# Transposing the exponentials of causal attention in two halves of 56 query rows, with padded queries and a new ranking of the work

## The chip, the cores and the metric

One NeuronCore of a Trainium2 chip runs the whole program. The metric is the device time of one execution in microseconds (us); the time before the change is 591.86 us, the median of three runs (591.3 to 592.4). One execution was also recorded by the hardware profiler, and the rows below come from it.

## The reference

Three stages follow one another: causal attention of 2 batches, 12 heads, 448 tokens and 64 features a head; a feed-forward layer with a rational function; and a gated feed-forward layer. The change sits in the first.

```python
scores = scale * np.matmul(q, k.transpose(0, 1, 3, 2))      # 448 x 448 a head
scores = np.where(mask, -1000000000.0, scores)              # causal
attn = np.exp(scores - np.max(scores, axis=-1, keepdims=True))
attn = attn / (np.sum(attn, axis=-1, keepdims=True) + 1e-09)
x = np.matmul(attn, v)                                      # 896 tokens x 768 in all
h = x @ w_in                                                # 768 x 2048
...
x = P(h) / (Q(h) + 1e-6) @ w_out                            # 2048 x 768
out = (sigmoid(x @ w_gate) * (x @ w_val)) @ w_out2          # 768 x 1536, 1536 x 768
```

## The kernel before, in words

**Attention** goes through 12 pairs of heads. A pair's queries and keys lie side by side as `qk` (128 partitions: 64 features of one head, 64 of the other), loaded on SP's queue at L558. The 448 queries of a pair are cut into NQ = 4 tiles t of CP = 112, and these into three groups k: tiles 0 and 1, tile 2, tile 3. Because of the causal mask tile t meets (t + 1) x 112 keys.

For each group, `scores` (L566) multiplies 112 queries with the keys for both heads j. A head's 64 features fill one half of the rows of TensorE (PE), so the two heads' matmuls stand in different halves by rows, and they write to two PSUM banks (`ps[:, 0]` and `ps[:, 1]`). A full fp32 matmul is issued as two instructions, each with a weight load of its own; a transpose as one. `maximum` (L579) is a DVE operation that adds the mask, writes the negated scores to SBUF as `e` and keeps their minimum; `exponentials` (L594) turns `e` into exponentials on ACT, with their sum. `turn` (L606) transposes `e` on PE block by block: for a tile t and a head j there are t + 1 blocks of 112 x 112, each one transpose (L615) over all 112 query rows, 20 for a pair. `copied` (L617) brings the transposed blocks from PSUM to SBUF as `pt`, on ACT for tile 2 and on DVE for the others. `values` (L646) multiplies `v` with `pt`; the two heads' results stand in two halves of PE's columns. `factors` (L627) spreads the inverse sums over the partitions with a matmul against the identity, also in two halves by columns, and `result` (L664) applies them. `xh` and `xl` (L667, L670) are two parts of the result whose sum has fp32's accuracy; the layers that follow multiply with fp32r parts, three matmuls for one product.

So PE works in three ways of division: rows (scores), columns (values and factors) and whole (the transposes, and all matmuls of the layers, L260 to L262, L319 to L321, L458 to L460 and L512 to L514).

**Order.** Nothing is ordered by hand. Each step is a `Job` with an engine, a cost, the jobs that it depends on and a rank. `in_turn` (L36) plays these jobs through with their costs, takes on each engine the ready job of the lowest rank, and writes the instructions out in that order; each engine then executes its own in that fixed order. Ranks come from `R` (offsets by kind of job, L692), costs from `C`, `EXP`, `MAX`, `COPY`, and the cost of a group's transposes is 0.2 us for each (t + 1) and 0.1 more (L728). `MODES` (L695) says which PE jobs divide the array; `switch` is the cost of going from one division to another, and it is 0 here. The first layer's products for the first batch (L260 to L262, then L319 to L321) are jobs of the same plan and fill gaps of the attention.

When the last job of the attention is done, `late` (L764) gives its SBUF and PSUM room to the layers: `room_b`, and the banks `ps_b` and `ps_d`. Weights come packed over SP's queue, are unpacked by ACT (L165, L169) and DVE (L172; L395 for the second layer), split on POOL (L180, L184, L423), and land in `room_a`, `room_b` and the `oh`/`ol` tiles. Ahead of the gated layer, DVE forms sums of the activations (L431 to L437, `act_sum`) and of the weights (L409 to L413, `weight_sums`), since that layer's products are formed with seven multiplications in place of eight.

Of the kernel before, what the change touches and what calls it, by code (L numbers as in the profile page):

```python
# [8 lines left out]
F32 = mybir.dt.float32  # L9
# [3 lines left out]
ALU = mybir.AluOpType  # L13
# [58 lines left out]
def tile_causal_attention__moe_rational__moe_glu(  # L72
# [13 lines left out]
    nc = tc.nc  # L86


    B, NP, P, _, S = qk.shape
    CP, NQ, _, D = v.shape[2:]  # L90
    DM = NP * P
    KC = DM // P

# [7 lines left out]
    MASK = -8.0e9  # L101
# [4 lines left out]
    const = ctx.enter_context(tc.tile_pool(name="const", bufs=1))  # L106
# [13 lines left out]
    for i in range(N_WARM):  # L120
        nc.tensor.matmul(warm[:, : 2 * P], ones[:, :P], ones, start=True, stop=True)

    ident = const.tile([P, P], F32, name="ident")
    make_identity(nc, ident)
    mask = const.tile([CP, S], F32, name="mask")
    nc.gpsimd.memset(mask, 0.0)
    nc.gpsimd.affine_select(
        out=mask[:, S - CP :],
        in_=mask[:, S - CP :],
        compare_op=ALU.is_ge,  # L130
        fill=MASK,
        base=0,
        pattern=[[-1, CP]],
        channel_multiplier=1,
    )
    a_sb = const.tile([P, 4], F32, name="a_sb")
    b_sb = const.tile([P, 2], F32, name="b_sb")
    nb = const.tile([P, 2], F32, name="nb")
# [14 lines left out]
    def weight(dst, src, nm, beside):  # L153

        f = src.shape[-1]
        raw = raws.tile([P, 2 * DM], U32, tag="raw", name=f"raw_{nm}")
        nc.sync.dma_start(out=raw.rearrange("p (c f) -> p c f", f=f), in_=src)
# [12 lines left out]
        yield  # L170
        val = raws.tile([P, DM], U32, tag="val", name=f"val_{nm}")
        nc.vector.scalar_tensor_tensor(  # L172
# [31 lines left out]
    def rows(tiles, key, src, f):  # L204


        def dst():
            tiles[key] = [
                wo_p.tile([P, DM], F32R, tag=t, name=f"{t}_{key[0]}{key[1]}_{key[2]}") for t in ("oh", "ol")
            ]  # L210
# [9 lines left out]
    BY_VECTOR = ("t3",)  # L220
    NO = DM // 2
    BY_POOL = ("in", "out")
    YW = 4 * DM
    ypools = [y_a, None]
# [83 lines left out]
    def out1_tile(c, b, e):  # L308
# [37 lines left out]
        "p6": ("s2", "t2", "B", True),  # L346
        "p7": ("s3", "t3", "C", True),
        "p5": ("s1", "t1", "D", True),
# [182 lines left out]
    nat = att.enter_context(tc.tile_pool(name="nat", bufs=3))  # L531
    xn_p = att.enter_context(tc.tile_pool(name="xn", bufs=1))
    ep = att.enter_context(tc.tile_pool(name="ep", bufs=2))
    pp = att.enter_context(tc.tile_pool(name="pp", bufs=2))
    st = att.enter_context(tc.tile_pool(name="st", bufs=3))
    ps_s = att.enter_context(tc.tile_pool(name="ps_s", bufs=2, space=PSUM))
# [6 lines left out]
    GROUPS = [(0, 1), (2,), (3,)]  # L543

    PK = NQ - 1
    NB = PK * PK + NQ

    def cols_of(t):

        grp = next(grp for grp in GROUPS if t in grp)  # L550
        return sum((k + 1) * CP for k in grp if k < t), (t + 1) * CP

    def load(n):
        b, hp = pairs[n]
        d = T[n] = {}
        u = f"{b}_{hp}"
        d["qk"] = nat.tile([P, 2, S], F32, tag="qk", name=f"qk_{u}")
        nc.sync.dma_start(out=d["qk"], in_=qk[b, hp])  # L558
        d["v"] = nat.tile([CP, NQ, 2, D], F32, tag="v", name=f"v_{u}")
        nc.sync.dma_start(out=d["v"], in_=v[b, hp])  # L560

        d["sum"] = st.tile([CP, NQ, 2], F32, tag="sum", name=f"sum_{u}")
        d["sc"] = st.tile([CP, NQ, 2], F32, tag="sc", name=f"sc_{u}")
        d["pt"] = pp.tile([CP, 2, NB, CP], F32, tag="pt", name=f"pt_{u}")

    def scores(n, k):  # L566

        d = T[n]
        ps = d["s", k] = ps_s.tile([CP, 2, 512], F32, tag="s", name=f"s_{n}_{k}")
        for t in GROUPS[k]:  # L570
            o, nk = cols_of(t)
            c = slice(t * CP, (t + 1) * CP)
            for j in range(2):
                r = slice(j * D, (j + 1) * D)
                nc.tensor.matmul(  # L575
                    ps[:, j, o : o + nk], d["qk"][r, 0, c], d["qk"][r, 1, :nk], start=True, stop=True
                )

    def maximum(n, k, t, j):  # L579
        d = T[n]  # L580
        o, nk = cols_of(t)
        e = d["e", t, j] = ep.tile([CP, nk], F32, tag=f"e{t}", name=f"e_{n}_{t}_{j}")
        nc.vector.tensor_tensor_reduce(  # L583
            e,
            d["s", k][:, j, o : o + nk],
            mask[:, S - nk :],
            op0=ALU.add,
            op1=ALU.min,
            scale=SCALE,
            scalar=3.0e38,  # L590
            accum_out=d["sc"][:, t, j : j + 1],
        )
# [12 lines left out]

    def turn(n, k):  # L606
        d = T[n]
        pz = d["p", k] = ps_s.tile([CP, 2, 512], F32, tag="s", name=f"p_{n}_{k}")
        for t in GROUPS[k]:
            o, _ = cols_of(t)  # L610
            for j in range(2):
                for kt in range(t + 1):
                    at = slice(o + kt * CP, o + (kt + 1) * CP)
                    e = d["e", t, j][:, kt * CP : (kt + 1) * CP]
                    nc.tensor.transpose(pz[:, j, at], e, ident[:CP, :CP])  # L615

    def copied(n, k, t):  # L617
        d = T[n]
        o, nk = cols_of(t)
        src = d["p", k][:, :, o : o + nk].rearrange("p j (k c) -> p j k c", c=CP)  # L620
        dst = d["pt"][:, :, t : t * (PK + 1) + 1 : PK]
        if t == 2:
            nc.scalar.copy(dst, src)
        else:
            nc.vector.tensor_copy(dst, src)

    def factors(n):  # L627

        d = T[n]
        d["r"] = ps_r.tile([P, 512], F32, tag="r", name=f"r_{n}")[:, :S]  # L630

        for i in range(NQ):
            for j in range(2):
                nc.tensor.matmul(
                    d["r"][j * D : (j + 1) * D, i * CP : (i + 1) * CP],
                    d["sum"][:, i, j : j + 1].to_broadcast([CP, D]),
                    ident[:CP, :CP],
                    start=True,
                    stop=True,
                )  # L640
# [5 lines left out]
    def values(n, kt):  # L646

        d = T[n]
        if kt == 0:
            d["x"] = ps_x.tile([P, 512], F32, tag="x", name=f"x_{n}")[:, :S]  # L650
        for j in range(2):
            nc.tensor.matmul(
                d["x"][j * D : (j + 1) * D, kt * CP :],
                d["v"][:, kt, j],
                d["pt"][:, j, kt * (PK + 1) : kt * PK + NQ].rearrange("p k c -> p (k c)"),
                start=(kt == 0),
                stop=(kt == NQ - 1),
            )
# [30 lines left out]

    NG = len(GROUPS)  # L690
    LA = 2
    R = dict(s=-41.5, turn=-13.0, r=-20.0, x=34.0, w=-3.5, max=-15.5, copy=-9.5, inv=7.0, xn=12.5, rout=-42.5, exp=6.75, hi=1.0, lo=4.5, e=3.0, p1=12.0, ts=0.0, th=-12.0, tl=0.0, wh=0.0, w2=-1.5, sum=6.0)  # L692
    C = dict(w_at=9.0, w_step=5.0, s=0.3, p=0.1, x=0.15, max=0.08, exp=0.19, switch=0.0, stay=0, copy=0.0, wa=0.1, wd=0.2, xn=0.1, rat=0.2)
    H = dict(PE=0.2, DVE=0.1, ACT=0.12, POOL=0.12, SP=0.03)
    MODES = {"s": "rows", "x": "columns", "r": "columns"}  # L695
    EXP = (0.39, 0.48, 0.57, 0.67)
    MAX = (0.28, 0.39, 0.51, 0.62)
    COPY = (0.39, 0.62, 0.70, 1.09)
# [1 line left out]
    for it in range(len(pairs) * NG + LA):  # L700
        n, k = divmod(it, NG)
        rank = it * NQ / NG
        if n < len(pairs):
            if k == 0:
# [5 lines left out]
                [("load", n), *freed_by("s")],  # L710
                rank + R["s"],
                scores,
# [3 lines left out]
            for t in GROUPS[k]:  # L716
                for j in both:
                    job(("max", n, t, j), "DVE", MAX[t] + C["max"], [("s", n, k), ("p", n - 1, k)], rank + R["max"], maximum, n, k, t, j)
                    job(("exp", n, t, j), "ACT", EXP[t] + C["exp"], [("max", n, t, j), ("r", n - 3)], rank + R["exp"], exponentials, n, t, j)
            freed["s"].append([("max", n, t, j) for t in GROUPS[k] for j in both])  # L720
        if it < LA:
            continue
        n, k = divmod(it - LA, NG)
# [1 line left out]
        job(  # L725
            ("p", n, k),
            "PE",
            sum(0.2 * (t + 1) for t in GROUPS[k]) + C["p"],  # L728
            [("exp", n, t, j) for t in GROUPS[k] for j in both] + freed_by("s"),
            rank + R["turn"],  # L730
            turn,
            n,
            k,
# [125 lines left out]
    at = {"end": 1000.0}  # L859
# [203 lines left out]
    u = 3  # L1063
# [30 lines left out]
def _laid_out(inputs):  # L1094
    import numpy as _np

    q, k, v = (inputs[n] for n in "qkv")
    b, h, s, d = q.shape
    t = [a.reshape(b, h // 2, 2, s, d).transpose(0, 1, 2, 4, 3).reshape(b, h // 2, 2 * d, s) for a in (q, k)]
    arrays = {  # L1100
        "qk": _np.ascontiguousarray(_np.stack(t, axis=3)),
        "v": _np.ascontiguousarray(v.reshape(b, h // 2, 2, 4, s // 4, d).transpose(0, 1, 4, 3, 2, 5)),
    }
    for name in _WEIGHTS:
        a = _np.ascontiguousarray(inputs[name])

        arrays[name] = a.view(_np.int64) if a.dtype == _np.float64 else a
    return arrays
# [22 lines left out]
```

## Time and profile before

| | us |
|---|---|
| median of three runs | 591.86 |
| the profiled execution, its own time | 591.18 |
| its span, from the first to the last instruction | 589.4 |
| PE busy | 576.6 |
| DVE busy | 441.7 |
| ACT busy | 388.3 |
| POOL busy | 320.6 |

The profiled execution's time holds 1.8 us around its span. A busy time counts the stretches in which at least one instruction of the engine is recorded as running. Matmuls overlap, and their ends are modelled, so two neighbouring starts tell more of PE's pace than a mean duration does. "PEld" is PE's weight load, which runs beside its matmuls; "issue" and a name behind "<-" in brackets say what ended an engine's idle time.

### The profile page before, as it was taken

Reading aid. Unit: us, or ns where it says so; the run is one execution under the profiler, and the core shown is the slowest. Engines: PE = TensorE matmul, PEld = TensorE weight load, DVE = VectorE, ACT = ScalarE, POOL = GpSimd, SP = SyncE. Lnnn points to the kernel's source line nnn. Section 1 sums busy time; section 2 is a strip of 40 time slices with the busy share of each in tenths; the row PEclk is TensorE's granted clock in tenths of the full one; section 3 lists DMA queues with packets and bytes.
Section 4 is the critical chain, followed back from the end, with each engine's and each line's share of the span. In section 5 each row is a group of like instructions: output and inputs, shape, how many; then the busy total and the mean of one; then the engine's idle time right before and its main releaser. Section 6 shows DMA issues by size and latency. Waiting matters only on the chain.

```text
span 589.4 us, 9051 instructions
## 1 busy us (share of the span) xinstructions
PE 576.6 (98%) x3244; PEld 497.3 (84%) x3244; DVE 441.7 (75%) x814; ACT 388.3 (66%) x767; POOL 320.6 (54%) x259
## 2 busy tenths in 40 slices
PE   7999999999999999999999979999999999999997
PEld 5556666689988998899889859999999999999996
DVE  4877889945978868789788987547668876857547
ACT  6888888957997673877677366677646566547210
POOL 0543341176647464636377887766658745756410
PEclk9999999999999999999999999999999999999999
DMA  7554450045333132513131103522443235441105
GB/s 247 191 197 126 147 179 17 2 158 165 108 107 108 54 108 73 191 59 107 55 108 54 55 0 108 160 87 82 154 131 137 85 131 161 125 138 60 53 2 187
DMA packets 35245, 65.07 MB, mean 110 GB/s; under 512 B 2368, under 2 KB 22592, under 8 KB 35200
## 3 DMA queue, kind: packets, MB, share of 16 engines
q1 hardware_dynamic: 35200, 64.50, 33.1%
q8 instruction: 25, 0.41, 0.3%
q14 instruction: 20, 0.16, 0.1%
HBM read 61.74 MB, written 2.75 MB: 109 GB/s over the span
## 4 chain that ended last, share of the span: by engine, by line
PE 66%; DVE 5%; ACT 3%; DMA 2%; POOL 1%; issue 1%; ACTq 0%; POOLq 0%; DVEq 0%
PE z L512 5%; PE z L514 5%; PE z L513 5%; PE o L320 5%; PE o L321 5%; PE o L319 5%; PE h L262 4%; PE h L261 4%; PE h L260 4%; PE u_C L458 2%; PE u_C L459 2%; PE u_C L460 2%; PE u_D L460 2%; PE u_D L459 2%; PE u_D L458 2%; PE u_A L460 2%
## 5 line engine op out<-in xcount | busy, mean ns | idle before, releaser
L184 POOL TENSOR_TENSOR ol_out<-val_out,oh_out 128x768 fp32r<-128x768 f32 x28 | 52.9, 1890 | 6.9 <-ACT oh_out L182 5.5
L512 PE MATMUL z<-oh_out,room_b 128*128 128x384 f32 x168 | 56.3, 335 | 0.0
L514 PE MATMUL z<-oh_out,room_b 128*128 128x384 f32 x168 | 56.1, 334 | 0.0
L513 PE MATMUL z<-ol_out,room_b 128*128 128x384 f32 x168 | 56.1, 334 | 0.0
L423 POOL TENSOR_TENSOR room_a<-val,room_a 128x384 fp32r<-128x384 f32 x30 | 34.1, 1146 | 40.4 <-ACT room_a L419 40.4
L597 ACT ACTIVATE e<-e,sc 112x112 f32<-112x112 f32 (+3 forms) x96 | 49.7, 520 | 6.5 <-DVE sc L583 6.4
L522 DVE TENSOR_TENSOR y<-y,z 128x384 f32<-128x384 f32 x84 | 43.5, 550 | 9.6 <-PE z L514 9.6
L583 DVE CUSTOM_DVE_ANT_0 e<-s,mask 112x112 f32<-112x112 f32 (+3 forms) x96 | 38.2, 445 | 14.4 <-PE s L575 13.1
L293 POOL TENSOR_TENSOR room_a<-t_h,room_a 128x384 fp32r<-128x384 f32 (+1 forms) x16 | 19.7, 1232 | 52.5 <-ACT room_a L291 46.0
L423 POOL TENSOR_TENSOR room_a<-raw,room_a 128x384 fp32r<-128x384 f32 x38 | 45.0, 1201 | 5.4 <-ACT room_a L419 5.4
L172 DVE SCALAR_TENSOR_TENSOR val_out<-raw_out 128x768 uint32<-128x768 uint32 x28 | 34.7, 1241 | 10.7 <-ACT raw_out L169 5.6
L395 DVE SCALAR_TENSOR_TENSOR val<-raw 128x768 uint32<-128x768 uint32 x24 | 25.1, 1044 | 22.3 <-ACT raw L392 19.1
L293 POOL TENSOR_TENSOR room_b<-t_h,room_b 128x512 fp32r<-128x512 f32 (+1 forms) x16 | 20.7, 1291 | 34.7 <-ACT room_b L291 33.8
L320 PE MATMUL o<-room_b,oh_out 128*128 128x512 f32 (+1 forms) x96 | 36.9, 385 | 0.7 <-POOL room_b L293 0.7
L319 PE MATMUL o<-room_b,oh_out 128*128 128x512 f32 (+1 forms) x96 | 36.9, 384 | 0.3 <-ACT room_b L291 0.3
L321 PE MATMUL o<-room_b,ol_out 128*128 128x512 f32 (+1 forms) x96 | 36.8, 384 | 0.0
L260 PE MATMUL h<-xh,room_a 128*128 128x448 f32 (+2 forms) x96 | 36.5, 380 | 0.0
L261 PE MATMUL h<-xl,room_a 128*128 128x448 f32 (+2 forms) x96 | 34.9, 364 | 0.0
L262 PE MATMUL h<-xh,room_a 128*128 128x448 f32 (+2 forms) x96 | 34.9, 363 | 0.0
L165 ACT ACTIVATE raw_out<-raw_out 128x768 f32<-128x768 f32 x28 | 25.6, 916 | 14.0 <-DMA raw_out<-in_moe_w_out_dram 13.8
L260 PE MATMUL h<-xh,room_b 128*128 128x384 f32 (+1 forms) x96 | 34.7, 362 | 0.0
L262 PE MATMUL h<-xh,room_b 128*128 128x384 f32 (+1 forms) x96 | 34.7, 362 | 0.0
(175 smaller groups left out, 1882.0 us busy)
## 6 DMA issues: line engine op xcount, KB each, us to landing
raw_out<-in_moe_w_out_dram SPq DMA_DIRECT2D x28, 768.0 KB, 4.3
raw_in<-in_moe_w_in_dram SPq DMA_DIRECT2D x16, 768.0 KB, 4.6
raw<-in_moe_w_gate_dram SPq DMA_DIRECT2D x24, 384.0 KB, 3.3
raw<-in_moe_w_val_dram SPq DMA_DIRECT2D x24, 384.0 KB, 4.0
qk<-in_qk_dram SPq DMA_DIRECT2D x12, 448.0 KB, 5.8
v<-in_v_dram SPq DMA_DIRECT2D x12, 224.0 KB, 3.6
out_dram<-y SPq DMA_DIRECT2D x14, 192.0 KB, 1.9
a_sb<-in_moe_a_dram SPq DMA_DIRECT2D x1, 2.0 KB, 7.7
```

Of the source, the lines that this page charges most:

```text
L184: nc.gpsimd.tensor_tensor(lo, vf, hi, op=ALU.subtract)
L260: nc.tensor.matmul(ps, hi[:, c, fs], xh[:, c, bs], start=(c == 0), stop=False)
L261: nc.tensor.matmul(ps, hi[:, c, fs], xl[:, c, bs], start=False, stop=False)
L262: nc.tensor.matmul(ps, lo[:, c, fs], xh[:, c, bs], start=False, stop=(c == KC - 1))
L319: nc.tensor.matmul(ps, hi[:, es], gh, start=(i == 0), stop=False)
L320: nc.tensor.matmul(ps, hi[:, es], gl, start=False, stop=False)
L321: nc.tensor.matmul(ps, lo[:, es], gh, start=False, stop=(i == NF - 1))
L423: nc.gpsimd.tensor_tensor(lo, halves[u, PRODUCTS[name][0]], hi, op=ALU.subtract)
L512: nc.tensor.matmul(ps, gh[:, ms], hi[:, ns], start=(u == us[0]), stop=False)
L513: nc.tensor.matmul(ps, gh[:, ms], lo[:, ns], start=False, stop=False)
L514: nc.tensor.matmul(ps, gl[:, ms], hi[:, ns], start=False, stop=(u == us[-1]))
L597: nc.scalar.activation(e, e, AF.Exp, bias=d["sc"][:, t, j : j + 1], scale=-1.0, accum_out=d["sum"][:, t, j : j + 1])
```

## The change

- A transpose of a block over 112 query rows becomes two, each over 56 rows: rows 0 to 55 and rows 64 to 119. The two stand in PE's two halves by rows. The first half writes to one PSUM bank of the tile, the second to the other; the two heads share each bank (`pz`, four slots of 256 columns). There are now 40 transposes for a pair in place of 20, and each passes 56 columns of the identity in place of 112.
- For that the second half's queries must begin at partition 64: a query tile has PQ = 120 rows, of which rows 56 to 63 are padding. The host writes zeros there; `qk` grows from 896 to 928 columns. Score weights, `e`, the sums and the mask have 120 rows; the mask is cut by two operations on POOL in place of one.
- `pt` keeps its size; its blocks are ordered by block, half, head and 56 queries in place of head and block, so `copied` reads four slots of PSUM, `values` reads runs of 56 columns, and `factors` multiplies with two runs of 56 columns of the identity.
- The plan: nearly all of the offsets `R` are changed, some costs `C` and hand-over times `H`, `switch` goes from 0 to 0.05, the transposes count as divided by rows like the scores, and their cost is 0.14 us for each (t + 1) and 0.1 more.

```diff
-    mask = const.tile([CP, S], F32, name="mask")
+    HQ = CP // 2
+    PQ = P // 2 + HQ
+    mask = const.tile([PQ, S], F32, name="mask")
     nc.gpsimd.memset(mask, 0.0)
-    nc.gpsimd.affine_select(
...
+    for h in range(2):
+        rows_of = slice(h * P // 2, min((h + 1) * P // 2, PQ))
+        nc.gpsimd.affine_select(
+            out=mask[rows_of, S - CP :],
...
-        d["qk"] = nat.tile([P, 2, S], F32, tag="qk", name=f"qk_{u}")
+        d["qk"] = nat.tile([P, NQ * PQ + S], F32, tag="qk", name=f"qk_{u}")
...
-        d["pt"] = pp.tile([CP, 2, NB, CP], F32, tag="pt", name=f"pt_{u}")
+        d["pt"] = pp.tile([CP, NB, 4, HQ], F32, tag="pt", name=f"pt_{u}")
...
-                    ps[:, j, o : o + nk], d["qk"][r, 0, c], d["qk"][r, 1, :nk], start=True, stop=True
+                    ps[:PQ, j, o : o + nk], d["qk"][r, c], d["qk"][r, NQ * PQ : NQ * PQ + nk], start=True, stop=True
...
     def turn(n, k):
         d = T[n]
-        pz = d["p", k] = ps_s.tile([CP, 2, 512], F32, tag="s", name=f"p_{n}_{k}")
+        pz = d["p", k] = ps_s.tile([P, 2, 512], F32, tag="s", name=f"p_{n}_{k}")
+        pz = pz.rearrange("p h (j c) -> p (h j) c", j=2)
         for t in GROUPS[k]:
-            o, _ = cols_of(t)
+            o = cols_of(t)[0] // 2
             for j in range(2):
                 for kt in range(t + 1):
-                    at = slice(o + kt * CP, o + (kt + 1) * CP)
-                    e = d["e", t, j][:, kt * CP : (kt + 1) * CP]
-                    nc.tensor.transpose(pz[:, j, at], e, ident[:CP, :CP])
+                    at = slice(o + kt * HQ, o + (kt + 1) * HQ)
+                    for h in range(2):
+                        r = slice(h * P // 2, h * P // 2 + HQ)
+                        e = d["e", t, j][r, kt * CP : (kt + 1) * CP]
+                        nc.tensor.transpose(pz[:CP, 2 * h + j, at], e, ident[r, r])
 
     def copied(n, k, t):
         d = T[n]
-        o, nk = cols_of(t)
-        src = d["p", k][:, :, o : o + nk].rearrange("p j (k c) -> p j k c", c=CP)
-        dst = d["pt"][:, :, t : t * (PK + 1) + 1 : PK]
+        o, nk = (c // 2 for c in cols_of(t))
+        pz = d["p", k].rearrange("p h (j c) -> p (h j) c", j=2)
+        src = pz[:CP, :, o : o + nk].rearrange("p h (k c) -> p h k c", c=HQ)
+        dst = d["pt"][:, t : t * (PK + 1) + 1 : PK].rearrange("p k h c -> p h k c")
...
-                    d["sum"][:, i, j : j + 1].to_broadcast([CP, D]),
-                    ident[:CP, :CP],
+                    d["sum"][:, i, j : j + 1].to_broadcast([PQ, D]),
+                    ident[:PQ].rearrange("p (h c) -> p h c", h=2)[:, :, :HQ],
...
-                d["pt"][:, j, kt * (PK + 1) : kt * PK + NQ].rearrange("p k c -> p (k c)"),
+                d["pt"][:, kt * (PK + 1) : kt * PK + NQ].rearrange("p k (h j) c -> p j k h c", j=2)[:, j],
...
-    R = dict(s=-41.5, turn=-13.0, r=-20.0, x=34.0, w=-3.5, max=-15.5, copy=-9.5, inv=7.0, xn=12.5, rout=-42.5, exp=6.75, hi=1.0, lo=4.5, e=3.0, p1=12.0, ts=0.0, th=-12.0, tl=0.0, wh=0.0, w2=-1.5, sum=6.0)
-    C = dict(w_at=9.0, w_step=5.0, s=0.3, p=0.1, x=0.15, max=0.08, exp=0.19, switch=0.0, stay=0, copy=0.0, wa=0.1, wd=0.2, xn=0.1, rat=0.2)
-    H = dict(PE=0.2, DVE=0.1, ACT=0.12, POOL=0.12, SP=0.03)
-    MODES = {"s": "rows", "x": "columns", "r": "columns"}
+    R = dict(s=-41.5, turn=-17.0, r=-20.0, x=34.0, w=-3.0, max=-17.0, copy=-9.5, inv=3.0, xn=10.5, rout=-39.0, exp=6.75, hi=9.5, lo=4.5, e=4.0, p1=18.0, ts=0.0, th=-8.0, tl=-0.5, wh=2.0, w2=-9.5, sum=7.0)
+    C = dict(w_at=9.0, w_step=5.5, s=0.33, p=0.1, x=0.15, max=0.08, exp=0.19, switch=0.05, stay=0.0, copy=0.0, wa=0.1, wd=0.23, xn=0.13, rat=0.15)
+    H = dict(PE=0.17, DVE=0.13, ACT=0.12, POOL=0.12, SP=0.03)
+    MODES = {"s": "rows", "p": "rows", "x": "columns", "r": "columns"}
...
-            sum(0.2 * (t + 1) for t in GROUPS[k]) + C["p"],
+            sum(0.14 * (t + 1) for t in GROUPS[k]) + C["p"],
```

## Rows read from the trace of the kernel before

**Rows 1.** The page: busy time of PE, and PE's granted clock in 40 slices.

```profile
PE   7999999999999999999999979999999999999997
PEclk9999999999999999999999999999999999999999
```

**Rows 2.** Stretches: length, busy us (instructions) of PE, PEld, DVE, ACT, POOL; clock; DMA.

```profile
20.00:60.00 40.00, 40.00 (x328) 24.31 (x328) 30.67 (x99) 34.68 (x100) 19.67 (x16) 1.00 0.58 196
60.00:120.00 60.00, 59.61 (x465) 37.99 (x467) 54.30 (x150) 51.17 (x135) 17.05 (x14) 1.00 0.24 78
120.00:140.00 20.00, 20.00 (x104) 18.41 (x100) 8.37 (x7) 11.86 (x19) 14.88 (x12) 1.00 0.56 172
...
70.00:80.00 10.00, 10.00 (x80) 6.67 (x80) 9.22 (x28) 9.40 (x27) 3.80 (x3) 1.00 0.54 180
110.00:120.00 10.00, 9.61 (x81) 6.05 (x81) 9.28 (x21) 8.89 (x20) 3.69 (x3) 1.00 0.01 2
```

**Rows 3.** Who waited for whom, 10 to 128 us: us in total, times, longest.

```profile
ACT pt L623 <- PE p L615: 8.3, 9, 1.6
DVE e L583 <- PE s L575: 8.0, 13, 1.1
```

**Rows 4.** PE's instructions in order of time: start, us from first to last, group.

```profile
38.72 0.98 PE L615 MATMUL p<-ident,e 112*112 112x112 f32 x8
39.63 0.99 PE L634 MATMUL r<-ident,sum 112*64 112x112 f32 x16
40.55 1.01 PE L575 MATMUL s<-qk 64*112 64x448 f32 x4
41.49 0.79 PE L615 MATMUL p<-ident,e 112*112 112x112 f32 x6
...
48.35 0.98 PE L615 MATMUL p<-ident,e 112*112 112x112 f32 x8
49.10 0.45 PE L260 MATMUL h<-xh,room_a 128*128 128x448 f32 x1
```

**Rows 5.** PE's weight loads by form: count, busy us, mean ns, idle before.

```profile
L615 PEld LDWEIGHTS p<-ident,e 112*112 112x112 f32 x240 | 23.1, 133 | 13.3 <-ACT e L597 5.2 <-issue 3.7 <-DVE pt L625 1.0
L575 PEld LDWEIGHTS s<-qk 64*112 64x112 f32 x192 | 12.3, 172 | 13.3 <-DVE sc L583 4.8 <-issue 3.5 <-DVE pt L625 2.2
L634 PEld LDWEIGHTS r<-ident,sum 112*64 112x64 f32 x192 | 9.4, 136 | 5.2 <-issue 1.2 <-ACT e L597 1.0 <-DVE sum L604 0.7
```

**Rows 6.** Loads of one transpose group in slices of 10 ns; (x) counts those running.

```profile
68.26:68.27 0.01, 0.01 (x1) 1.00 0.00 0
...
68.31:68.32 0.01, 0.01 (x2) 1.00 1.67 358
...
68.41:68.42 0.01, 0.01 (x2) 1.00 3.49 1434
```

**Rows 7.** The same slices for loads of one group of scores (L575).

```profile
62.96:62.97 0.01, 0.01 (x2) 1.00 0.00 0
...
63.06:63.07 0.01, 0.01 (x4) 1.00 0.00 0
```

**Rows 8.** DVE's copies of transposed blocks, 5 to 122 us: count, busy us, mean ns.

```profile
L625 DVE COPY pt<-p 112x896 f32<-112x896 f32 x12 | 13.1, 1090 | 4.9 <-PE p L615 4.9
L625 DVE COPY pt<-p 112x448 f32<-112x448 f32 x12 | 7.4, 614 | 0.0
L625 DVE COPY pt<-p 112x224 f32<-112x224 f32 x12 | 4.6, 387 | 0.3 <-PE p L615 0.2
```

**Rows 9.** The chain that ended last: start, us, what.

```profile
124.56 0.85 POOL room_b L180
```

**Rows 10.** Stretches ahead of the gated layer, columns as in Rows 2.

```profile
340.00:345.00 5.00, 3.54 (x18) 2.92 (x17) 5.00 (x7) 4.20 (x9) 4.80 (x5) 1.00 0.00 0
345.00:350.00 5.00, 3.39 (x16) 2.42 (x14) 4.37 (x6) 2.34 (x3) 3.83 (x3) 1.00 0.00 0
```

**Rows 11.** The page: loads of queries and keys on SP's queue.

```profile
qk<-in_qk_dram SPq DMA_DIRECT2D x12, 448.0 KB, 5.8
```

More of the change, by code (lines that the diff above doesn't have):

```diff
@@ L86, in tile_causal_attention__moe_rational__moe_glu @@
     nc = tc.nc
-    B, NP, P, _, S = qk.shape
+    B, NP, P, _ = qk.shape
     CP, NQ, _, D = v.shape[2:]
+    S = CP * NQ
     DM = NP * P
@@ L124, in tile_causal_attention__moe_rational__moe_glu @@
     make_identity(nc, ident)
-    mask = const.tile([CP, S], F32, name="mask")
+    HQ = CP // 2
+    PQ = P // 2 + HQ
+    mask = const.tile([PQ, S], F32, name="mask")
     nc.gpsimd.memset(mask, 0.0)
-    nc.gpsimd.affine_select(
[L128 to L135, printed above, removed]
+    for h in range(2):
+        rows_of = slice(h * P // 2, min((h + 1) * P // 2, PQ))
+        nc.gpsimd.affine_select(
+            out=mask[rows_of, S - CP :],
+            in_=mask[rows_of, S - CP :],
+            compare_op=ALU.is_ge,
+            fill=MASK,
+            base=h * HQ,
+            pattern=[[-1, CP]],
+            channel_multiplier=1,
+        )
     a_sb = const.tile([P, 4], F32, name="a_sb")
@@ L560, in load @@
         nc.sync.dma_start(out=d["v"], in_=v[b, hp])
-        d["sum"] = st.tile([CP, NQ, 2], F32, tag="sum", name=f"sum_{u}")
-        d["sc"] = st.tile([CP, NQ, 2], F32, tag="sc", name=f"sc_{u}")
-        d["pt"] = pp.tile([CP, 2, NB, CP], F32, tag="pt", name=f"pt_{u}")
+        d["sum"] = st.tile([PQ, NQ, 2], F32, tag="sum", name=f"sum_{u}")
+        d["sc"] = st.tile([PQ, NQ, 2], F32, tag="sc", name=f"sc_{u}")
+        d["pt"] = pp.tile([CP, NB, 4, HQ], F32, tag="pt", name=f"pt_{u}")
     def scores(n, k):
         d = T[n]
-        ps = d["s", k] = ps_s.tile([CP, 2, 512], F32, tag="s", name=f"s_{n}_{k}")
+        ps = d["s", k] = ps_s.tile([P, 2, 512], F32, tag="s", name=f"s_{n}_{k}")
         for t in GROUPS[k]:
             o, nk = cols_of(t)
-            c = slice(t * CP, (t + 1) * CP)
+            c = slice(t * PQ, (t + 1) * PQ)
             for j in range(2):
@@ L581, in maximum @@
         o, nk = cols_of(t)
-        e = d["e", t, j] = ep.tile([CP, nk], F32, tag=f"e{t}", name=f"e_{n}_{t}_{j}")
+        e = d["e", t, j] = ep.tile([PQ, nk], F32, tag=f"e{t}", name=f"e_{n}_{t}_{j}")
         nc.vector.tensor_tensor_reduce(
             e,
-            d["s", k][:, j, o : o + nk],
+            d["s", k][:PQ, j, o : o + nk],
             mask[:, S - nk :],
@@ L1098, in _laid_out @@
     b, h, s, d = q.shape
-    t = [a.reshape(b, h // 2, 2, s, d).transpose(0, 1, 2, 4, 3).reshape(b, h // 2, 2 * d, s) for a in (q, k)]
+    q, k = (a.reshape(b, h // 2, 2, s, d).transpose(0, 1, 2, 4, 3).reshape(b, h // 2, 2 * d, s) for a in (q, k))
+    half = s // 8
+    wide = _np.zeros((b, h // 2, 2 * d, 4, d + half), q.dtype)
+    for i in range(2):
+        wide[..., i * d : i * d + half] = q.reshape(b, h // 2, 2 * d, 4, 2, half)[..., i, :]
     arrays = {
-        "qk": _np.ascontiguousarray(_np.stack(t, axis=3)),
+        "qk": _np.concatenate([wide.reshape(b, h // 2, 2 * d, -1), k], axis=3),
         "v": _np.ascontiguousarray(v.reshape(b, h // 2, 2, 4, s // 4, d).transpose(0, 1, 4, 3, 2, 5)),
```

## The prediction, made before the changed kernel ran

> **What bounds the kernel now.** I read the page's slices first: PE is 90% busy or more in 37 of 40 slices, at a granted clock of full speed throughout [rows 1]. That alone proves little, because ends of matmuls are modelled, so I went on to the attention, where the change lies, some 5 to 122 us. By stretches, PE is busy for all of 20 to 60 us and for 59.61 of the 60 us after that; ACT has 34.68 of the first 40, DVE 54.30 of the last 60 [rows 2]. The waits say which of the three leads: ACT's copies stand idle for the transposes, 8.3 us in all, and DVE's maxima for the scores, 8.0 us [rows 3]. So the followers wait for PE, though not by much: the fullest 10 us of ACT hold 9.40, of DVE 9.28 [rows 2]. PE bounds the attention, with DVE and ACT close behind.
>
> Last, PE's own pace, from starts in order of time. Eight transposes followed by a product of the layer start 0.75 us before it, 94 ns each; eight followed by the factors, which divide the array by columns, take 0.91 us [rows 4]. The same work costs 0.16 us more where the next group divides the array otherwise: that is the price of a change of division.
>
> **Part 1, the transposes.** There are 240, at 94 ns: 22.6 us of PE [rows 4, 5]. What sets the 94 ns? In one group the second load starts 50 ns after the first, the third 100 ns after the second [rows 6]: a load can follow in about 50 ns, and from then on the pass of 112 columns holds it up. The mean load tells the same, 133 ns where the scores' load of equally many columns takes 172 [rows 5]. So both the pass and the load matter to a half:
> - The pass is half as long, 47 ns, and two halves by rows can run beside each other, as two heads' scores do: their loads start in twos, within the same 10 ns [rows 7].
> - The load is not shorter: each half still loads 112 columns, 50 ns if it stays a transpose's load and the two halves load together. The scores' second pair of loads follows the first by 100 ns [rows 7]; if a half-height transpose loads at that speed, the pair costs 100 ns.
>
> A pair therefore costs between 47 ns (both at once) and 94 to 100 ns (in turn, or with the scores' load). I take 60: the transposes' own row is nearer than the scores', and the pair issues one load and one matmul more, for which I allow some 6 ns each, since loads of one pair start less than 10 ns apart [rows 7]. That removes 240 x 34 ns = 8.2 us of PE, with the ends at 11.3 us and nothing.
>
> Here a rule speaks against the change. The eight passes of the factors, in pairs by columns, are 16 matmuls in 0.92 us, a change of division included: (0.92 - 0.16) / 16 = 47 ns a matmul [rows 4]. The Trainium skill says (TensorE: Matmul & The Clock Gate, "Wait — 56ns, not 53.3ns?") that one way of decoding costs some 62 ns for each matmul and binds once the array's work is shorter. By that an estimate for the pair is 124 ns, and Part 1 would add 7.2 us; the 47 ns of this trace are below such a floor.
>
> **Part 2, changes of division.** Scores and transposes now divide the array alike. Going through PE's groups from 4 to 122 us in that view, I count 21 places where transposes follow scores, as at 40.55 and 41.49, and 7 the other way; those 28 changes go. In 12 places transposes border on a product of the layer, as at 48.35 and 49.10, and there a change is new [rows 4]. In the old order that is 16 fewer, 16 x 0.16 = 2.6 us; with the new ranks it can be anything from none to all 28, 4.5 us.
>
> **Part 3, the small terms.** The scores load 120 columns for 112: at 100 ns for 112 [rows 7], 7 ns more, and only where the pass is no longer than the load, in the 2 matmul steps of tile 0 of 12 pairs: 0.2 us. The loads of queries and keys grow by 16 of 448 KB, 3.6% of 5.8 us [rows 11]: three buffers hide that except at the start, where I put 0.1 us. The mask's second operation on POOL lies beside that first load; uncovered it would cost a fraction of a microsecond once. `copied` has twice as many runs, each half as long. From 224 to 896 elements a copy grows by 703 ns for 672 elements, 1.01 ns each in the first step and 1.06 in the second, while its runs go from 2 to 8 [rows 8]: a run costs nothing that shows, so I put 0; the cover to look at would be DVE, which has none to spare. For `values` and `factors` (runs of 56, 120 rows) I put 0; nothing in the trace reads such runs on PE, and 10% more on the factors alone, 0.76 us a pair [rows 4], would be 0.9 us, which I leave to the range.
>
> **Sum for PE:** 8.2 + 2.6 - 0.3 = 10.5 us less, out of about 117.
>
> **What of it reaches the end.** PE's queue is fixed, so it gains only as far as its suppliers keep up. If ACT and DVE keep all their work there and run no fuller than their fullest 10 us, the first 40 us cannot go below 34.68 / 0.94 = 36.9, and the next 60 not below 54.30 / 0.93 = 58.4: 4.7 us gained. If the plan moves what is not attention (the unpacking of weights, the rational function) behind its end, where DVE has 8.37 and ACT 11.86 of 20 us [rows 2], all 10.5 are gained. New offsets for these kinds of work do exist in the change, in both directions. I take 7.0, between the two and somewhat nearer the lower. Behind the attention nothing absorbs it: the chain that ended last enters the split of the next weights on POOL at 124.56 us, whose room is given free by the attention's end [rows 9], and from there runs through weights to PE. It starts that much earlier. What is late next is DVE within the attention: copies and maxima.
>
> The profiled execution, 591.18, becomes 584.2. The median of the runs shown is 0.7 us above it, so I expect a median of **584.9 us**; with the ends of the terms, this case reaches from 580 to 588.
>
> **Rivals.**
> 1. *The transposes gain nothing* (the pair stays near 94 ns, because loads go at the scores' speed or in turn). For: rows 7 are the only loads of half height. Against: rows 5 and 6, where a transpose's load is quicker. Left are 2.3 us of Part 2 and 3, of which about 2 arrive: 589.9. Chance 0.13.
> 2. *Each half pays its own way, and the change is slower.* If half-height transposes do not run beside each other, each costs its pass and the issue of its load and matmul, 47 + 17 = 64 ns by the bounds above, the pair 128, so Part 1 adds 8.2 us, and with Part 2 the end lies 5.6 us later: 597.5. It decides from 105 ns a pair on, where Part 1 outweighs Part 2's 2.6 us. For: twice as many instructions. Against: rows 7, two heads side by side, and the factors' 47 ns. Chance 0.08. (The skill's 62 ns, named above, would end here too, near 596.)
> 3. *The new ranks lose it later.* Ahead of the gated layer DVE is full, 9.37 us of 10, and PE stands idle for 3.1 us [rows 10]. The offsets of that layer's weights (w2, wh) and of its sums (th) are moved. DVE's work there is fixed; if unpacking is now put in front of the sums, that wait can double or more, 4 us: 588.9. It could also shrink; I know of no row that decides. Chance 0.12.
> 4. *Everything arrives*: the pair at 47 ns, no new changes of division and work moved out of DVE's way, 13 to 15 us: 578. Chance 0.05.
>
> **The numbers.** The forecast has the remaining 0.62. A difference under 0.2%, 1.2 us, is about what a measurement of this kernel cannot tell from none. Faster by more: nearly all of the forecast (0.60), most of rivals 1 and 3 (0.09 and 0.07) and rival 4: 0.81. Slower: rival 2 and the bad ends of 1 and 3, 0.11. Within: 0.08. The range from 579.5 to 590.5 holds the forecast but for its edges and most of rivals 1 and 3, and leaves out rivals 2 and 4 and some of 1 and 3, about 2 in 10.
>
> **What would show it.** Part 1: a group of 16 half transposes of tile 3 ahead of scores should take some 0.5 us from its start to the next; 0.75 says rival 1, 1.0 rival 2; their loads should start in twos. Part 2: no 0.16 us between scores and transposes, and one before a product of the layer. The share that arrives: attention's last `values` some 7 us earlier, PE's waits for DVE and ACT longer than now, DVE above 93% from 60 us on. Rival 3: PE's idle time ahead of the gated layer, 3.1 us now. The forecast is wrong if the pairs are fast and the attention ends where it did: then DVE or ACT had been the bound.

## The result and the profile after

The changed kernel takes 584.06 us (median of four runs, 583.45 to 584.88), beside 592.13 us for the kernel before in the same measurement: a ratio of 0.9865, with a 95% interval from 0.9845 to 0.9886. The forecast was 584.9 us. The profiled execution has a span of 583.1 us, 6.3 us less than before. In the profiles of this study the first `values` starts anywhere from 15.8 to 17.1 us, so I compare the attention by the distance from the first to the last start of `values`.

The first view is that of the instructions of one line, `values`, in the changed kernel: durations in ns (least, middle, most), first and last start in us, forms.

```profile
L661 PE MATMUL x<-pt,v x192: 258/425/591, 16.8 to 113.2; 112*64 112x448 f32 x48, 112*64 112x336 f32 x48, 112*64 112x224 f32 x48, 112*64 112x112 f32 x48
```

The same line before:

```profile
L652 PE MATMUL x<-pt,v x192: 259/424/590, 16.1 to 120.1; 112*64 112x448 f32 x48, 112*64 112x336 f32 x48, 112*64 112x224 f32 x48, 112*64 112x112 f32 x48
```

From first to last it was 104.0 us, now it is 96.4: the attention is 7.6 us shorter, and that is nearly the whole result. Both kernels have 27 of the layer's products in that stretch, so no product was pushed out of it.

PE's groups in order of time, the changed kernel (start, us from first to last):

```profile
30.84 1.02 PE L580 MATMUL s<-qk 64*120 64x448 f32 x4
31.70 0.54 PE L623 MATMUL p<-ident,e 56*112 56x56 f32 x12
32.17 1.54 PE L661 MATMUL x<-pt,v 112*64 112x448 f32 x8
...
34.32 0.49 PE L623 MATMUL p<-ident,e 56*112 56x56 f32 x12
34.74 0.99 PE L643 MATMUL r<-ident,sum 120*64 120x112 f32 x16
...
36.90 0.60 PE L623 MATMUL p<-ident,e 56*112 56x56 f32 x16
37.43 0.47 PE L265 MATMUL h<-xh,room_a 128*128 128x448 f32 x1
...
63.19 0.65 PE L623 MATMUL p<-ident,e 56*112 56x56 f32 x16
63.67 0.97 PE L580 MATMUL s<-qk 64*120 64x448 f32 x4
```

Sixteen half transposes ahead of scores take 0.48 us, 60 ns a pair, where eight whole ones took 0.91 us ahead of the factors [rows 4], and as much ahead of scores. Ahead of a product of the layer they take 0.53 us, where eight whole ones took 0.75. Scores of 448 columns followed by transposes take 0.86 us in place of 0.94 [rows 4]. A part of these times belongs to changes of division at either end of a group; the last section takes them apart.

The weight loads of the group at 36.90, in slices of 10 ns, with the count of those running in brackets:

```profile
36.90:36.91 0.01, 0.01 (x2) 1.00 0.00 0
...
36.96:36.97 0.01, 0.01 (x4) 1.00 0.00 0
...
37.01:37.02 0.01, 0.01 (x6) 1.00 0.00 0
```

They start in twos, 50 to 60 ns apart, as the scores' loads do at 100 ns [rows 7]; a whole transpose's loads came one at a time, 100 ns apart [rows 6]. So the two halves do run side by side, and a half's load keeps the transposes' short time: its mean is 132 ns, as the whole one's was 133 [rows 5].

```profile
L623 PEld LDWEIGHTS p<-ident,e 56*112 56x112 f32 x480 | 17.8, 132 | 11.5 <-ACT e L602 4.2 <-issue 3.2 <-DVE pt L634 1.3
```

Stretches of the changed kernel, with the columns of [rows 2]:

```profile
20.00:60.00 40.00, 40.00 (x472) 25.79 (x468) 34.73 (x117) 38.26 (x107) 21.61 (x18) 1.00 0.62 208
60.00:120.00 60.00, 57.59 (x574) 39.46 (x570) 52.53 (x139) 52.03 (x135) 19.29 (x16) 1.00 0.31 101
...
70.00:80.00 10.00, 9.87 (x105) 6.56 (x106) 9.86 (x29) 8.96 (x24) 3.40 (x4) 1.00 0.69 237
80.00:90.00 10.00, 9.94 (x114) 6.97 (x114) 9.86 (x27) 8.78 (x25) 1.92 (x2) 1.00 0.12 39
90.00:100.00 10.00, 9.60 (x95) 6.48 (x90) 9.89 (x27) 8.78 (x26) 1.92 (x3) 1.00 0.01 2
```

ACT is now 96% busy from 20 to 60 us, DVE 99% from 70 to 100 us, and from 60 us on PE is idle for 2.41 us in place of 0.39 [rows 2]. PE's waits that name DVE (us in total, times, longest):

```profile
PE s L580 <- DVE sc L588: 3.1, 5, 0.8
...
PE x L661 <- DVE xn L674: 0.7, 1, 0.7
PE r L643 <- DVE sum L609: 0.6, 1, 0.6
PE p L623 <- DVE pt L634: 0.4, 1, 0.4
```

Of the 3.1 us, 2.3 lie at the start of the attention, where the kernel before has 1.8. From 20 us on DVE holds PE up for 2.1 us in all, 0.3 before.

DVE's copies cost what they did [rows 8], with twice as many runs:

```profile
L634 DVE COPY pt<-p 112x896 f32<-112x896 f32 x12 | 13.0, 1084 | 1.7 <-PE p L623 1.7
...
L634 DVE COPY pt<-p 112x448 f32<-112x448 f32 x12 | 7.4, 615 | 0.0
...
L634 DVE COPY pt<-p 112x224 f32<-112x224 f32 x12 | 4.6, 386 | 0.0
```

Ahead of the gated layer PE is idle for 3.96 us between 330 and 345 us and for nothing until 365, in place of 3.1 us from 340 to 350 us and some more behind it [rows 10]. The stretches after:

```profile
330.00:345.00 15.00, 11.04 (x52) 9.22 (x51) 13.62 (x16) 9.74 (x20) 12.46 (x11) 1.00 0.00 0
345.00:365.00 20.00, 20.00 (x100) 18.21 (x99) 14.18 (x19) 13.19 (x23) 16.21 (x15) 1.00 0.26 80
```

### The profile page after: what moved, and what is told of

It is laid out like the page before. It is cut to its first block, busy times and chain, and to the rows that moved or that the text cites. A ratio compares the mean times of both kernels' runs of the same rounds, so it can differ in the third digit from the quotient of the medians.

```text
span 583.1 us, 9528 instructions
## 1 busy us (share of the span) xinstructions
PE 567.4 (97%) x3484; PEld 493.5 (85%) x3484; DVE 442.2 (76%) x814; ACT 387.6 (66%) x767; POOL 317.3 (54%) x260
## 4 chain that ended last, share of the span: by engine, by line
PE 75%; DVE 15%; DMA 3%; ACT 3%; POOL 2%; issue 2%; DVEq 0%; ACTq 0%
PE h L265 5%; PE o L325 5%; PE o L326 5%; PE o L324 5%; PE h L266 5%; PE h L267 5%; PE z L517 4%; PE z L518 4%; PE z L519 4%; PE s L580 4%; DMA raw_in<-in_moe_w_in_dram 3%; PE x L661 3%; PE u_C L463 2%; PE u_C L464 2%; PE u_C L465 2%; PE u_A L465 2%
## 5 line engine op out<-in xcount | busy, mean ns | idle before, releaser
L602 ACT ACTIVATE e<-e,sc 120x112 f32<-120x112 f32 (+3 forms) x96 | 49.9, 524 | 9.0 <-DVE sc L588 8.9
L298 POOL TENSOR_TENSOR room_a<-t_h,room_a 128x384 fp32r<-128x384 f32 (+1 forms) x16 | 18.4, 1148 | 61.6 <-ACT room_a L296 38.8
L588 DVE CUSTOM_DVE_ANT_0 e<-s,mask 120x112 f32<-120x112 f32 (+3 forms) x96 | 38.1, 444 | 10.9 <-PE s L580 10.5
L580 PE MATMUL s<-qk 64*120 64x112 f32 (+3 forms) x192 | 32.5, 439 | 3.1 <-DVE sc L588 3.1
L265 PE MATMUL h<-xh,room_b 128*128 128x384 f32 (+1 forms) x96 | 34.7, 362 | 0.0
L266 PE MATMUL h<-xl,room_b 128*128 128x384 f32 (+1 forms) x96 | 34.7, 362 | 0.0
```

The lines of the kernel that those rows point to most:

```text
L265: nc.tensor.matmul(ps, hi[:, c, fs], xh[:, c, bs], start=(c == 0), stop=False)
L266: nc.tensor.matmul(ps, hi[:, c, fs], xl[:, c, bs], start=False, stop=False)
L580: nc.tensor.matmul(ps[:PQ, j, o : o + nk], d["qk"][r, c], d["qk"][r, NQ * PQ : NQ * PQ + nk], start=True, stop=True)
```

## The experiments

Theory 1 is the prediction's: PE bound the attention, half transposes make PE's queue shorter, and DVE and ACT take a part of that back. Its rivals: the new plan brings the gain (theory 2 below); a half is cheaper only for its fewer columns; DVE or ACT bound the attention all along. Every run was timed side by side with the kernel before; "values" is the distance from the first to the last start of `values` in the run's profile.

| run | us | ratio to before (95%) | values, us |
|---|---|---|---|
| before | 591.9 to 592.7 | | 104.0 |
| changed kernel, first time | 584.06 | 0.9865 (0.9845 to 0.9886) | 96.4 |
| changed kernel again | 585.30 | 0.9890 (0.9867 to 0.9913) | 96.3 |
| halves, old plan | 584.14 | 0.9864 (0.9846 to 0.9883) | 97.3 |
| whole transposes, new ranks | 596.20 | 1.0069 (1.0046 to 1.0091) | 110.3 |
| halves in turn | 587.74 | 0.9932 (0.9909 to 0.9956) | 99.0 |
| changed, no addition | 583.00 | 0.9852 (0.9832 to 0.9873) | 94.8 |
| the same again | 583.51 | 0.9854 (0.9834 to 0.9874) | 94.9 |
| before, no addition | 591.88 | 1.0000 (0.9987 to 1.0013) | 103.9 |
| halves, old plan, no addition | 585.42 | 0.9894 (0.9876 to 0.9911) | 96.8 |
| changed, no inverse | 583.66 | 0.9857 (0.9839 to 0.9875) | 94.9 |
| changed, no sums | 584.54 | 0.9870 (0.9849 to 0.9892) | 96.5 |
| before, no sums | 591.88 | 0.9995 (0.9982 to 1.0007) | 104.1 |
| changed, no sums, no inverse | 583.22 | 0.9848 (0.9828 to 0.9867) | 95.4 |

**Code or plan?** First the halves in the old order, with `R`, `C` and all other numbers of the plan as before:

```diff
-    H = dict(PE=0.17, DVE=0.13, ACT=0.12, POOL=0.12, SP=0.03)
-    MODES = {"s": "rows", "p": "rows", "x": "columns", "r": "columns"}
+    H = dict(PE=0.2, DVE=0.1, ACT=0.12, POOL=0.12, SP=0.03)
+    MODES = {"s": "rows", "x": "columns", "r": "columns"}
...
-            sum(0.14 * (t + 1) for t in GROUPS[k]) + C["p"],
+            sum(0.2 * (t + 1) for t in GROUPS[k]) + C["p"],
```

> The changed kernel with the plan's numbers of before (offsets, costs, hand-over times, 0.2 us for each block, no division by rows), so that all instructions stand in the old order and only the transposes, the padding and what reads them are new. Theory 1 (PE's pace: pairs of half transposes at 60 ns for 94, fewer changes of division): most of the gain comes without the new plan, 585 to 588 us, ratio to before 0.988 to 0.993; the plan adds the rest. Theory 2 (the new plan brings the gain): about 592, ratio 0.998 to 1.002. A group of 16 half transposes ahead of scores should again take about 0.5 us.

It takes 584.14 us: all of the gain, with nothing of the new plan. Then the other part alone, the kernel before with the new `R`, `C` and `H`:

```diff
-    H = dict(PE=0.2, DVE=0.1, ACT=0.12, POOL=0.12, SP=0.03)
+    H = dict(PE=0.17, DVE=0.13, ACT=0.12, POOL=0.12, SP=0.03)
...
```

> The kernel before with the new plan's offsets, costs and hand-over times, but whole transposes at 0.2 us a block. Theory 1: no gain of its own, 591 to 594 us, ratio 0.998 to 1.004. Theory 2: 584 to 588, ratio 0.987 to 0.993.

596.20 us, 0.7% slower than before, which neither theory had put there. The new ranks are no gain by themselves, and they are bad for whole transposes: `values` then take 110.3 us from first to last. By PE's starts that order has 119 changes of division up to the last `values`, where the old one has 111, and one product of the layer more in the stretch; the rest of the 6 us was not taken apart. With half transposes the two plans cannot be told apart by time (584.14 beside 584.06 and 585.30 us). Theory 2 has fallen.

**Side by side, or just shorter?** The loop over the halves is put outside, so that neighbours share one half of the array, and one PSUM bank:

```diff
-            for j in range(2):
-                for kt in range(t + 1):
-                    at = slice(o + kt * HQ, o + (kt + 1) * HQ)
-                    for h in range(2):
-                        r = slice(h * P // 2, h * P // 2 + HQ)
+            for h in range(2):
+                r = slice(h * P // 2, h * P // 2 + HQ)
+                for j in range(2):
+                    for kt in range(t + 1):
+                        at = slice(o + kt * HQ, o + (kt + 1) * HQ)
```

> The changed kernel with the loop over the two halves put outside the loops over heads and blocks of a tile, so that neighbouring transposes share one half of the array and one PSUM bank. Theory 1 holds that the price of 60 ns a pair comes from two halves running side by side: without that a pair should cost about 100 ns, a group of 16 about 0.8 us, PE has some 9 us more, and the time goes back to 589 to 593 us (ratio to before 0.995 to 1.002). If a half is simply cheaper because it passes half as many columns, a group of 16 stays near 0.5 us and the time near 584.

PE's groups of that run, in order of time:

```profile
34.77 0.65 PE L623 MATMUL p<-ident,e 56*112 56x56 f32 x12
35.35 0.99 PE L643 MATMUL r<-ident,sum 120*64 120x112 f32 x16
...
37.50 0.86 PE L623 MATMUL p<-ident,e 56*112 56x56 f32 x16
38.29 0.47 PE L265 MATMUL h<-xh,room_a 128*128 128x448 f32 x1
```

Sixteen take 0.79 us, 49 ns each, where the changed kernel's take 0.53. The time goes back to 587.74 us, some 3.7 us of the 8, in the place of the 5 to 9 expected. But the halves are not strictly in turn here. These lines count the transposes of the group at 37.50 that have begun by 37.70, 37.90 and 38.20 us:

```profile
37.49:37.70 0.21, 0.20 (x4) 1.00 0.00 0
37.49:37.90 0.41, 0.40 (x11) 1.00 0.00 0
37.49:38.20 0.71, 0.70 (x16) 1.00 0.28 61
```

The same for the group at 36.90 of the changed kernel:

```profile
36.89:37.10 0.21, 0.20 (x8) 1.00 0.00 0
36.89:37.30 0.41, 0.40 (x16) 1.00 0.01 5
```

Four begin in the first 0.2 us, 54 ns apart, seven in the next 0.2 us and five after that. All eight of one half were written ahead of the other eight, and yet in the middle of the group two begin within a few ns of each other: there, too, both halves of the array are at work. A half that has nothing beside it takes 54 ns, as long as a whole pair takes in the changed kernel. Sixteen strictly in turn would take, by an estimate from these starts, 16 x 54 ns = 0.86 us and 0.09 for the change of division ahead of the layer, more than the 0.75 of eight whole ones. So the 3.7 us are a lower bound of what it is worth that the halves run beside each other: a half is not cheaper just for its fewer columns. Whether the array's halves or the banks must alternate is not shown, since the edit changes both.

**Who takes the rest back?** In the next runs DVE and then ACT have less to do, in both kernels. First the addition is taken out of `inverses`:

```diff
-        nc.vector.tensor_scalar_add(rs, rs, 1e-9)
```

> The changed kernel without the addition of 1e-9 to the sums of exponentials (that part of the reference is left out; a sum is at least 1, so fp32 holds the same number without it). One DVE operation fewer for each of 12 pairs, 3 to 4 us of DVE busy time in the attention, nothing else changed. If DVE bounds the second half of the attention now (DVE busy 98% from 70 to 105 us), the time falls by 1 to 3 us, to 581 to 583. If PE still bounds it, it stays within 0.5 us of 584.

583.00 us, and 583.51 when timed again, beside 584.06 and 585.30 for the changed kernel; the intervals overlap, so I call it some 1 us ahead and no more. The stretch of `values` is 1.6 us shorter, and that came out twice (94.8 and 94.9, beside 96.4 and 96.3). The same line taken out of the kernel before:

> The kernel before without the addition of 1e-9 to the sums (left out here as in the run of the changed kernel without it). Theory 1 says that PE bound the attention before the change and that DVE became its second bound only with it: then the same relief of DVE, 3 to 4 us of its busy time, is worth nothing or little here, ratio to before 0.998 to 1.001. If DVE bound the attention all along, it is worth as much as in the changed kernel or more, about 1 to 2 us, ratio 0.996 to 0.998.

591.88 beside 591.93 us: nothing. This is the clearest pair of the study: the same operation, 3.7 us of DVE's busy time before the change and 2.2 behind it (3 to 4 had been put for both), is worth 0.1 us of the attention before the change and 1.6 behind it. DVE did not bound it then. The same line taken out of the halves with the old plan:

> The halves with the old plan's numbers, and without the addition of 1e-9. Theory 1: the plan is worth nothing either way, so this comes out within 1 us of the changed kernel without the addition, 582.5 to 584. If the new plan is what lets a lighter DVE pay, it stays at 584 or above.

585.42 us, so outside the forecast of theory 1 and, by what was written down, for the rival: a lighter DVE pays only in the new order. `values` are 0.5 us closer than with the addition, 1.6 in the new plan. So the plan is not worth nothing either way: without the addition the new order is some 2 us ahead of the old one, and the intervals just miss each other. One run of the old order carries this, so I would not build on its size. Next, in the changed kernel, the reciprocal is taken out too:

```diff
-        nc.vector.tensor_scalar_add(rs, rs, 1e-9)
-        nc.vector.reciprocal(rs, rs)
```

> The changed kernel without the addition and without the reciprocal (the division by the sums is left out; the sums are multiplied in instead). DVE has 6 us less in the attention. If DVE holds back what PE gained, the time falls further than without the addition alone, to 580.5 to 582.5. If what is left is PE's own pace, it stays at 583 to 584.

This kernel leaves the division out and multiplies by the sums. 583.66 us, beside 585.30 for the changed kernel timed with it, and `values` at 94.9 us as without the addition alone. Twice the relief gives no more: by what was written down, what is left is not DVE's load.

The changed kernel, with no edit, was timed beside these:

> The changed kernel as it stands, beside the others of this call: 583.5 to 585 us, ratio to before 0.985 to 0.988, as in the first measurement.

585.30 us, just outside what was written. Then ACT: `accum_out` is taken from the exponentials, so ACT forms no sums, and POOL writes ones in their place:

```diff
+        nc.gpsimd.memset(d["sum"], 1.0)
...
-            e, e, AF.Exp, bias=d["sc"][:, t, j : j + 1], scale=-1.0, accum_out=d["sum"][:, t, j : j + 1]
+            e, e, AF.Exp, bias=d["sc"][:, t, j : j + 1], scale=-1.0
```

> The changed kernel without the sums that ACT forms beside each exponential (left out; POOL writes ones in their place), so 96 read-outs of ACT's accumulator, some 190 ns each, fall away; all else and the order are as they were. Theory 1 holds that ACT (96% busy from 20 to 60 us) holds back what PE gained in the first half of the attention, as DVE does in the second: the time falls by 2 to 5 us, to 579 to 582.5. If what is left is PE's own pace, it falls by less than 1 us.

584.54 us: no gain. A stretch of that run, columns as in [rows 2]:

```profile
20.00:60.00 40.00, 40.00 (x463) 25.87 (x458) 34.35 (x116) 35.61 (x68) 21.80 (x23) 1.00 0.61 207
```

ACT is down from 38.26 to 35.61 us, and PE did no more in that time: 463 matmuls begun or running, as against 472. ACT at 96% was no bound.

The same edit in the kernel before:

> The kernel before without the same sums (left out, ones in their place). Theory 1: PE bound the attention then, so the relief of ACT is worth little, ratio to before 0.997 to 1.001. If ACT bound it all along, it is worth as much as in the changed kernel, ratio under 0.996.

591.88 us, nothing either.

And both edits of the changed kernel, no sums and no inverse, at once:

> The changed kernel without ACT's sums and without DVE's addition and reciprocal (sums and division left out). If ACT and DVE together are what PE's gain is lost to, this gives more than either alone: PE's full 11 us less than before, 579 to 581, ratio 0.978 to 0.982. If it stays near 583, something else holds it.

583.22 us, not the 579 to 581 of theory 1, and `values` 95.4 us, no closer than with the addition alone taken out. So the load of DVE and ACT together holds back some 1 to 1.6 us, not all that is missing.

The last pair of heads shows where most of the rest lies. PE from its last transposes to the last `values`, in the changed kernel:

```profile
108.48 0.65 PE L623 MATMUL p<-ident,e 56*112 56x56 f32 x16
109.68 0.99 PE L643 MATMUL r<-ident,sum 120*64 120x112 f32 x16 [0.55 <-DVE sum L609]
111.37 2.11 PE L661 MATMUL x<-pt,v 112*64 112x448 f32 x16 [0.70 <-DVE xn L674]
```

The same place in the kernel before:

```profile
115.98 0.98 PE L615 MATMUL p<-ident,e 112*112 112x112 f32 x8
116.73 0.45 PE L319 MATMUL o<-room_a,oh_out 128*128 128x448 f32 x1
...
117.51 0.99 PE L634 MATMUL r<-ident,sum 112*64 112x112 f32 x16
118.33 2.06 PE L652 MATMUL x<-pt,v 112*64 112x448 f32 x16
```

Before, a product of the layer fills the gap and PE waits for nothing. Now nothing fills it: PE stands idle until DVE has inverted the sums, and again until DVE is done with `result`. DVE in order of time:

```profile
108.68 0.62 DVE L294 SCALAR_TENSOR_TENSOR t_h<-d_h,t_h 128x448 f32<-128x448 f32 x1
109.23 0.16 DVE L608 TENSOR_SCALAR sum<-sum 120x8 f32<-120x8 f32 x1
...
109.55 1.04 DVE L634 COPY pt<-p 112x896 f32<-112x896 f32 x1
110.50 0.61 DVE L674 TENSOR_TENSOR xn<-xn,x 128x448 f32<-128x448 f32 x1
```

The sums come behind the rational function, `result` behind a copy of 1.04 us. The transposes and the factors take 1.20 and 1.69 us to the next group's start, where the same groups take 0.53 and 0.82 unhindered: 1.5 us of waiting. Without the addition both waits are still there:

```profile
PE x L660 <- DVE xn L673: 0.7, 1, 0.7
PE r L642 <- DVE sum L608: 0.6, 1, 0.6
```

With all of the relief it is one wait, of 1.5 us, for `result`. This is a place in a fixed order, which a lighter load does not move; no run tried another order there. The candidate once more:

> The changed kernel without the addition of 1e-9 once more, the candidate for a version ahead of both kernels: 582 to 584 us, ratio to before 0.983 to 0.988.

583.51 us. Of the versions that keep all that fp32 can hold (a sum of exponentials is at least 1, and 1e-9 beside it is lost), the changed kernel without the addition has the lowest medians.

## Why the prediction was right, step by step

- **What bounds the kernel.** Right, and now shown: the kernel before gains nothing from a lighter DVE or a lighter ACT (ratios 1.0000 and 0.9995), and 8 us from a shorter queue on PE.
- **Part 1, 60 ns a pair.** Measured 60 ns ahead of scores, 54 from pair to pair inside a group. The argument from the transposes' own short load holds. (Whole ones start 96 ns apart; the 94 is the mean of a group with a long first and a short last step.) By the 62 ns a matmul that the Trainium skill gives for one way of decoding (TensorE: Matmul & The Clock Gate, "Wait — 56ns, not 53.3ns?"), an estimate for the group of sixteen is 0.99 us. That rule, which spoke against the change, does not bind here: 16 matmuls in 0.48 us are 30 ns each. The bound of 94 to 100 ns for a pair in turn was near the truth, if low: a half with nothing beside it takes 54 ns, so 108 for two.
- **Part 2, 16 changes of division fewer at 0.16 us.** The count was right, and the sum was near, but there is not one price. Behind whole transposes a change costs 0.16 us, behind halves 0.09 to 0.10, and between scores and transposes its absence saves 0.08 to 0.09 of the scores' time. So the changes ahead of `values`, counted as unchanged, became cheaper too, and that was not in the sum.
- **Sum for PE, 10.5 us.** From the run in the old order, group by group against the kernel before, by the middle of each kind: 19 groups of 12 ahead of `values`, 0.72 to 0.43 us, 5.5 us; 3 ahead of the layer, 0.56 to 0.42, 0.4; tile 3's 12 groups, five 0.91 to 0.48 ahead of scores, five 0.75 to 0.58, two 0.91 to 0.55, 3.7 together; 21 scores ahead of transposes at 0.08 to 0.09, 1.8; 4 products of the layer ahead of transposes, 0.1 longer each. That is 11.0 us.
- **What arrives, 7.0 us.** Measured 7.6 us in `values` and 8.1 in the medians. The number was right, its reason was half wrong, and so that it came this close is in part luck. The floor of 4.7 us rested on ACT and DVE running no fuller than their fullest 10 us. Both now run fuller, DVE at 9.89 of 10, and ACT was no floor at all. Nor did it take a plan that moves other work behind the attention: the old order gains 6.7 us in `values`, and in time as much as the new one. If PE's groups gain in the new order the 11.0 us that they gain in the old one, 3.4 us did not arrive. DVE's addition accounts for 1.6, shown by taking it out. The last pair's two waits account for 1.5; that is read from the traces, and no run removes them. Some 0.3 us stay open.
- **Rivals.** 1 fell by the pace of the pairs, 2 by the loads in twos. 3 fell too: PE's idle time ahead of the gated layer is 3.96 us between 330 and 365 us, 3.81 before (1.46 and 2.35 in the same two stretches), and the old plan's time is the same. The 17 ns that rival 2 puts on the issue of a load and a matmul stand in no row; the two of a pair start mostly 3 to 10 ns apart. The prediction had not asked what the new ranks do to whole transposes: they make the kernel 0.7% slower.

## What to carry to other kernels

Where PE is the bound and a transpose has room in rows, cut it in two halves that alternate between the array's halves and write to two banks: passes of half as many columns, two at a time, make a pair cost 60 ns in place of 94. One half with nothing beside it costs 54 here, so two that never overlap would gain nothing in pace. Judge by starts, not by busy time, and test a full engine by taking work from it: an engine at 96% may be waited for by nobody. Try a plan's numbers apart from the code they came with; here, with the addition in place, they were worth nothing with it and cost 0.7% without it. And look at the last round of a pipeline by itself: what is left there can be a wait for one step in a fixed order, which no lighter load removes.

## What was not expected of the hardware

A change of the array's division has no single price. Where the last transpose of a group starts tells it. For the whole transposes at 38.72 (begun by 39.43 and by 39.45 us):

```profile
38.71:39.43 0.72, 0.71 (x7) 1.00 0.36 77
38.71:39.45 0.74, 0.73 (x8) 1.00 0.39 86
```

For the halves at 34.32 of the changed kernel:

```profile
34.31:34.58 0.27, 0.26 (x10) 1.00 0.27 110
34.31:34.61 0.30, 0.29 (x12) 1.00 0.24 99
```

The factors follow at 39.63 [rows 4], 0.19 us behind the last whole transpose, and at 34.74, 0.14 us behind the last half. With no change of division, a product of the layer follows a whole transpose after 0.03 us, and scores follow a half after 0.05. So the change costs 0.16 us behind whole transposes and 0.09 to 0.10 behind halves. On the way in it is alike: the first step of a group behind factors is 0.05 us longer than the others in both kernels. The Trainium skill says that a change of tiling mode drains the engine (TensorEngine Tiling (Array Packing), Key Properties); the trace agrees that it costs something, and its numbers say that how much depends on what runs before it. Why half transposes leave more cheaply is open.

The run in turn shows another thing. By the spacing of the starts, the transposes of one half of the array begin beside the last three or four of the other half, though they were all written behind them.
